# Mixing and gated MLP on one core: own buffers for the first x pieces, the second-stage table in six groups, and the exponent clamps moved from VectorE to ScalarE

## The chip, the core and the metric

One core of a Trainium2 chip. The metric is the device time of one execution in microseconds (us), which for one core is the time of that core. Executions of one kernel mostly agree within 0.3%. Medians are given, and ratios with a 95% interval.

Names: PE is TensorE's matmul, PEld its weight load, DVE is VectorE, ACT is ScalarE, POOL is GpSimd, SP is the engine that issues most DMAs. The granted clock is the share of its full clock that TensorE had in a stretch, as the profile records it. L392 is line 392 of the kernel concerned, so the same statement has different numbers in different kernels.

## The reference, cut to what matters

```python
X = np.fft.fft(x, axis=1)          # x: (8, 3008, 256) float32
X = np.fft.fft(X, axis=2)
h = X.real.astype(np.float32).reshape(24064, 256) @ w_in    # w_in: (256, 2048), float64
g = h * np.clip(h + 3.0, 0.0, 6.0) / 6.0
out = (g @ w_out).astype(np.float32)                        # w_out: (2048, 256), float64
```

The weights arrive as float64. The kernel doesn't compute in it: it takes the two 32-bit halves of each number and builds a float32 with integer operations. That is "the conversion" below: 16 tiles of 128x512.

## The kernel before

The batches go in four pairs. Of a pair, 32 rows come in eight chunks of four and are folded with their mirror rows (fetched by a gather, an indirect DMA), go through a first Fourier stage on TensorE (stage 1), are copied to z on ScalarE, stored to DRAM, read back as g, and go through stage 2 and the gated MLP. Later pairs do their first stage beside the MLP of the pair ahead. The first pair has nothing to hide behind, and its start also has to convert the weights. ScalarE and VectorE run their operations in the order in which the program emits them; the traces below show it (in the changed kernel a ScalarE operation whose input is ready at 85.3 us starts at 89.33, behind two copies emitted before it).

```python
PR = 94                                   # partitions of an x tile
xpool = ...tile_pool(name="xpool", bufs=2)

def load_x(pr, c):                        # one chunk
    xt = xpool.tile([PR, 2 * XC, D], F32, tag="x", name="xt")
    nc.gpsimd.dma_start(out=xt[:, 0:n, :], in_=rows[...])             # rows
    nc.gpsimd.indirect_dma_start(out=xt[:, XC:, :]..., in_=x_r, ...)  # mirror rows: the gather
...
def narrow(st, o):                        # the conversion, all on VectorE
    ts(top[:], hi, 0xFFFFF, 0x100000, op0=AL.bitwise_and, op1=AL.bitwise_or)
    ts(low[:], lo, 8, 0xFFFFFF, op0=AL.logical_shift_right, op1=AL.bitwise_and)
    stt(frac[:], low[:], 2.0 ** -24, top[:], op0=AL.mult, op1=AL.add)
    ts(ex[:], hi, 20, 0x7FF, op0=AL.logical_shift_right, op1=AL.bitwise_and)
    ts(ex[:], ex[:], 1023.0 - 127.0, 0.0, op0=AL.subtract, op1=AL.max)   # clamp
    ts(ex[:], ex[:], 255.0, 2.0 ** 23, op0=AL.min, op1=AL.mult)          # clamp
    stt(ex[:], hi, -2 ** 31, ex[:], op0=AL.bitwise_and, op1=AL.bitwise_or)   # sign
    stt(o, frac[:], 2.0 ** -20, ex[:].bitcast(F32), op0=AL.mult, op1=AL.mult)
...
for c in range(NXC):                      # eight chunks of the first pair
    for part, eng in enumerate((nc.gpsimd, nc.vector)):
        fold(first, c, part, eng)         # part 0 on GpSimd, part 1 (y) on VectorE
    if c + 2 < NXC: load_x(first, c + 2)
    for i in range(XC // 2):
        stage1(first, c, i)               # TensorE matmul, then nc.scalar.copy(z, ps)
    narrow_w_in(c)
    if c + 2 < NWI: load_w_in(c + 2)
    if c % 2: fold_w_in(c // 2)           # TensorE: w_in folded with the dimension transform
# ... then two w_out conversions; the other six beside the first eight gate steps
```

Of the kernel before, what the change touches and what calls it, by code (L numbers as in the profile page):

```python
# [7 lines left out]
F32 = mybir.dt.float32  # L8
# [40 lines left out]
def kernel(  # L49
# [30 lines left out]
    xpool = ctx.enter_context(tc.tile_pool(name="xpool", bufs=2))  # L80
# [21 lines left out]
    T = consts.tile([P, 2, NK1, 2, N2], F32, name="T")  # L102
# [14 lines left out]



    def load_x(pr, c):  # L120
        xt = xpool.tile([PR, 2 * XC, D], F32, tag="x", name="xt")
# [3 lines left out]
        if n < XC:  # L125
# [3 lines left out]
            out=xt[:, XC:, :].rearrange("p n d -> p (n d)"), out_offset=None, in_=x_r,  # L129
            in_offset=bass.IndirectOffsetOnAxis(ap=IX[:, i:i + 1], axis=0),  # L130
        )
        pr.x[c] = xt

    def fold(pr, c, part, eng):
        xt = pr.x[c]
        n = XC if c < NXC - 1 else XC - 1
        a, r = xt[:, 0:n, :], xt[:, 2 * XC - 1:2 * XC - 1 - n:-1, :]
# [7 lines left out]
        lo, hi = xt[:, 0:XC, 1:P], xt[:, 0:XC, D - 1:P:-1]  # L145
# [3 lines left out]
        if n < XC:  # L149
            h = xt[:, XC, :]  # L150
            tt(y[:, XC, 1:P], h[:, 1:P], h[:, D - 1:P:-1], op=AL.add)
            tt(y[:, XC, P + 1:D], h[:, 1:P], h[:, D - 1:P:-1], op=AL.subtract)
            eng.tensor_copy(y[:, XC, 0:P + 1:P], h[:, 0:P + 1:P])
            eng.tensor_copy(y[:, n, 0:P + 1:P], xt[:, n, 0:P + 1:P])
# [46 lines left out]
    def stage2(pr, gr, i):  # L201
# [5 lines left out]
        for u in range(2):  # L207
            kk = 2 * i + u
            for blk in range(2):
                nc.tensor.matmul(ps[:, blk, 2 * u:2 * u + 2], g[:, kk, blk * P:(blk + 1) * P],  # L210
                                 T[:, blk, gr * 2 * KK + kk], start=True, stop=True)
        nc.scalar.copy(pr.q[gr][:, :, 4 * i:4 * i + 4, :], ps[:])

    def stage2n_mul(pr, gr):

        shape = [P, 2 * KK, 2 * N2]
        m = spool.tile(shape, F32, tag="m", name="m")
        t0 = T[:, 0, gr * 2 * KK:(gr + 1) * 2 * KK].rearrange("p k b n -> p k (b n)")
        nc.gpsimd.tensor_tensor(m[:], t0, pr.g[gr][:, :, P:P + 1].to_broadcast(shape), op=AL.mult)
        pr.pr[gr] = m  # L220

    def stage2n_sum(pr, gr):
        m = pr.pr.pop(gr)
        ps = bank([P, 2 * TB], "ps3")
        nc.tensor.matmul(ps[:], ones[:], m[:].rearrange("p k n -> p (k n)"), start=True, stop=True)  # L225
# [128 lines left out]
    for c in range(2):  # L354
        load_x(first, c)
# [7 lines left out]
    def load_w(src, dst):  # L363
        if not wide:
            nc.sync.dma_start(out=dst, in_=src)
            return None
        st = wpool.tile([P, 2 * WB], I32, tag="st", bufs=3, name="st")
# [6 lines left out]
    def narrow(st, o):  # L374


        if st is None:
            return
        words = st[:].rearrange("p (n two) -> p n two", two=2)
        lo, hi = words[:, :, 0], words[:, :, 1]  # L380
        ts, stt = nc.vector.tensor_scalar, nc.vector.scalar_tensor_tensor
        top = wpool.tile([P, WB], I32, tag="top", name="top")
        low = wpool.tile([P, WB], I32, tag="low", name="low")
        ex = wpool.tile([P, WB], I32, tag="ex", name="ex")
        frac = wpool.tile([P, WB], F32, tag="frac", name="frac")
        ts(top[:], hi, 0xFFFFF, 0x100000, op0=AL.bitwise_and, op1=AL.bitwise_or)
        ts(low[:], lo, 8, 0xFFFFFF, op0=AL.logical_shift_right, op1=AL.bitwise_and)  # L387
        stt(frac[:], low[:], 2.0 ** -24, top[:], op0=AL.mult, op1=AL.add)  # L388
        ts(ex[:], hi, 20, 0x7FF, op0=AL.logical_shift_right, op1=AL.bitwise_and)
        ts(ex[:], ex[:], 1023.0 - 127.0, 0.0, op0=AL.subtract, op1=AL.max)  # L390
        ts(ex[:], ex[:], 255.0, 2.0 ** 23, op0=AL.min, op1=AL.mult)
        stt(ex[:], hi, -2 ** 31, ex[:], op0=AL.bitwise_and, op1=AL.bitwise_or)  # L392
        stt(o, frac[:], 2.0 ** -20, ex[:].bitcast(F32), op0=AL.mult, op1=AL.mult)

    w_in = {}

    def load_w_in(j):
        n, i = j // 2, j % 2
        w = wpool.tile([P, WB], F32, tag="w", bufs=5, name="w_in")
        w_in[n, i] = w, load_w(moe_w_in[i * P:(i + 1) * P, n * WB:(n + 1) * WB], w[:])  # L400

    def narrow_w_in(j):
        w, st = w_in[j // 2, j % 2]
        narrow(st, w[:])


    w_out = {}

    def load_w_out(j):
        w = wpool.tile([P, WB], F32, tag="w", bufs=5, name="w_out")  # L410
        rows = moe_w_out[2 * j * P:2 * (j + 1) * P, :].rearrange("(c p) d -> p c d", p=P)
        w_out[j] = w, load_w(rows, w[:].rearrange("p (c d) -> p c d", c=2))

    def narrow_w_out(j):
        w, st = w_out[j]
        narrow(st, w[:])

    def mix_w_out(j):
        bs = [w_out[j + i * (NWO // 2)][0][:].rearrange("p (c q h e) -> h p c q e", c=2, h=2, e=DH) for i in range(2)]
# [14 lines left out]
    for j in range(2):  # L434
        load_w_in(j)
    for b in range(2):
        nc.vector.memset(T[(1 - b) * N2:(2 - b) * N2, :, :, b], 0.0)
        nc.scalar.dma_start(out=T[b * N2:(b + 1) * N2, :, :, b], in_=c_stage2)
# [3 lines left out]
    def fold_w_in(n):  # L442

        cs = slice(n * 512, (n + 1) * 512)
        for blk in range(2):
            ps = bank([P, 512], "wps")
            for i in range(2):
                nc.tensor.matmul(ps[:], C[:, i, blk * P:(blk + 1) * P], w_in[n, i][0][:],
# [3 lines left out]
        for j in range(512 // P):  # L452
            for i in range(2):
                nc.tensor.matmul(ps[:, j:j + 1], w_in[n, i][0][:, j * P:(j + 1) * P], C[:, i, D:D + 1],
                                 start=(i == 0), stop=(i == 1))
        nc.scalar.copy(WN[:, n * (512 // P):(n + 1) * (512 // P)], ps[:, 0:512 // P])

    for c in range(NXC):
        for part, eng in enumerate((nc.gpsimd, nc.vector)):
            fold(first, c, part, eng)  # L460
        if c + 2 < NXC:
            load_x(first, c + 2)
        for i in range(XC // 2):
            stage1(first, c, i)
        narrow_w_in(c)
        if c + 2 < NWI:
            load_w_in(c + 2)
        if c % 2:
            fold_w_in(c // 2)
    ORDER = [0, NWO // 2, 1, NWO // 2 + 1, 2, NWO // 2 + 2, 3, NWO // 2 + 3]  # L470
    for j in ORDER[0:2]:
        load_w_out(j)
# [6 lines left out]
    for j in range(2):  # L479
        narrow_w_out(ORDER[j])  # L480
        load_w_out(ORDER[j + 2])
    mix_w_out(0)
    starting[0] = False

# [4 lines left out]
    def beside(p):  # L489
# [6 lines left out]
        if p == 0:  # L496
            for j in range(2, NWO):
                put(j - 2, narrow_w_out, ORDER[j])
                if j + 2 < NWO:
                    put(j - 2, load_w_out, ORDER[j + 2])  # L500
# [63 lines left out]
def _tables(B, S, D):  # L564
# [14 lines left out]
    for b in range(2):  # L579
# [21 lines left out]
        "c_stage2": t.reshape(N2, 2, NK1, N2).astype(np.float32),  # L601
# [33 lines left out]
```

## Time and profile before

| | before |
|---|---|
| median, us | 2097.04 (2094.95 to 2097.82) |
| last z copy of the first pair starts at | 102.85 |
| first gate step (the first `s` on VectorE) at | 120.09 |
| last weight conversion ends at | 191.93 |
| TensorE full from | 196.84 |

I call the time up to the first gate step "half one" and the eight slow gate steps after it "half two".

The next lines are from the list of waits of the first 125 us (who waited for whom: us in total, times, the longest). They are what makes half one long: GpSimd waits for the gathers, VectorE for GpSimd.

```profile
DVE y L146 <- POOL xt L141: 40.9, 6, 15.5
POOL xt L140 <- DMA xt<-in_x_dram,IX: 40.2, 6, 15.3
```

The stretches between GpSimd's take-up of chunks 0, 2, 4 and 6 (length, then busy us and counts of PE, PEld, DVE, ACT and POOL, the granted clock, the DMA share and GB/s): each pair of chunks costs 21 us, in which no engine is busy for more than 14.05.

```profile
23.57:44.72 21.15, 12.91 (x22) 4.82 (x22) 14.05 (x22) 3.19 (x6) 9.35 (x9) 1.00 0.57 152
44.72:65.82 21.10, 13.71 (x39) 6.27 (x38) 13.62 (x22) 3.96 (x8) 9.63 (x8) 0.68 0.56 159
65.82:86.60 20.78, 12.96 (x32) 5.51 (x31) 11.31 (x22) 3.51 (x7) 10.01 (x10) 0.67 0.57 158
```

### The profile page before, as it was taken

How to read it: one execution, taken by the hardware profiler on the slowest of the kernel's cores; microseconds unless marked ns; L12 is line 12 of the kernel's file. 1: busy time of each engine (PE TensorE's matmuls, PEld its weight loads, DVE VectorE, ACT ScalarE, POOL GpSimd, SP SyncE). 2: the span in 40 equal slices, each digit the busy share in tenths (PEclk: the TensorE clock that was granted, in tenths of full speed). 3: DMA queues.
4: the chain of work that ended last, by engine and by line, in shares of the span. 5: the costliest groups of instructions: out<-in, count | busy, mean ns of one | idle time of the engine just before them, and what ended most of it. 6: DMA issues, size and time to landing. Idle time of an engine off the chain costs nothing.

```text
span 2095.7 us, 28082 instructions
## 1 busy us (share of the span) xinstructions
PE 1985.9 (95%) x9136; PEld 1698.7 (81%) x9136; DVE 1495.8 (71%) x2768; ACT 671.6 (32%) x1157; POOL 1474.1 (70%) x1637
## 2 busy tenths in 40 slices
PE   3666999999999999999999999999999999999997
PEld 1355888888888888888888888888888888888886
DVE  4588676777677677667677667777677777777775
ACT  1122333333333333333333333333333333333332
POOL 3333887788667788778767787787866766766765
PEclk9678999999999999999999999999999999999999
DMA  6430121112101112112101111111020010010000
GB/s 160 133 110 10 43 54 48 50 37 49 28 21 34 43 33 61 47 38 52 35 21 30 42 38 43 42 51 47 23 48 11 14 26 21 16 26 21 16 16 19
DMA packets 163377, 86.81 MB, mean 41 GB/s; under 512 B 138496, under 2 KB 151040, under 8 KB 163232
## 3 DMA queue, kind: packets, MB, share of 16 engines
q1 hardware_dynamic: 128896, 58.71, 11.4%
q0 software_dynamic: 28160, 24.73, 4.4%
q10 hardware_dynamic: 6176, 1.57, 0.4%
q8 instruction: 74, 1.21, 0.3%
q14 instruction: 71, 0.58, 0.1%
HBM read 47.65 MB, written 37.22 MB: 40 GB/s over the span
## 4 chain that ended last, share of the span: by engine, by line
PE 88%; DVE 5%; DMA 4%; ACT 1%; POOL 1%; issue 1%; SPq 0%; DVEq 0%; POOLq 0%; ACTq 0%
PE acc L308 52%; PE v L254 15%; PE u L254 15%; DMA xt<-in_x_dram,IX 3%; PE ps L210 2%; PE ps L182 2%; DVE a L286 1%; PE ps L225 1%; ACT t L283 1%; DVE u L267 1%; DVE s L259 0%; DVE frac L388 0%; DVE low L387 0%; DMA g<-zd 0%; DVE ex L392 0%
## 5 line engine op out<-in xcount | busy, mean ns | idle before, releaser
L298 POOL TENSOR_TENSOR c<-a 128x512 f32<-128x512 f32 (+1 forms) x384 | 479.2, 1248 | 447.2 <-DVE a L286 257.2
L308 PE MATMUL acc<-c,G 128*128 128x256 f32 (+1 forms) x3072 | 714.0, 375 | 0.0
L308 PEld LDWEIGHTS acc<-c,G 128*128 128x128 f32 x3072 | 579.7, 191 | 73.9
L283 ACT ACTIVATE t<-u,half 128x512 f32<-128x512 f32 (+2 forms) x416 | 272.2, 654 | 1102.5 <-DVE u L267 1090.8
L259 DVE SCALAR_TENSOR_TENSOR s<-qn,WN,u 128x256 f32<-128x256 f32 x768 | 334.7, 477 | 365.1 <-PE u L254 364.5
L308 PE MATMUL acc<-a,G 128*128 128x256 f32 (+1 forms) x2304 | 557.5, 379 | 0.0
L308 PEld LDWEIGHTS acc<-a,G 128*128 128x128 f32 x2304 | 439.8, 192 | 58.7
L254 PE MATMUL v<-q,W 128*128 128x256 f32 x1536 | 402.3, 385 | 31.7 <-DVE a L286 31.7
L254 PE MATMUL u<-q,W 128*128 128x256 f32 x1536 | 395.0, 379 | 0.0
L254 PEld LDWEIGHTS v<-q,W 128*128 128x128 f32 x1536 | 292.6, 192 | 80.3 <-issue 35.3
L254 PEld LDWEIGHTS u<-q,W 128*128 128x128 f32 x1536 | 287.9, 190 | 65.8 <-issue 20.7
L286 DVE SCALAR_TENSOR_TENSOR a<-t,u 128x512 f32<-128x512 f32 (+2 forms) x416 | 266.2, 646 | 99.2 <-ACT t L283 94.0
L298 POOL TENSOR_TENSOR c<-a,c 128x256 f32<-128x256 f32 (+1 forms) x384 | 276.2, 719 | 30.1
L298 POOL TENSOR_TENSOR c<-c,a 128x256 f32<-128x256 f32 (+1 forms) x384 | 274.9, 716 | 30.1
L267 DVE TENSOR_TENSOR u<-s,v 128x512 f32<-128x512 f32 (+1 forms) x384 | 263.0, 685 | 41.1 <-PE v L254 1.3
L283 ACT ACTIVATE t<-v,half 128x512 f32<-128x512 f32 (+1 forms) x384 | 256.9, 669 | 5.5 <-DVE v L273 4.5
L273 DVE TENSOR_TENSOR v<-v,s 128x512 f32<-128x512 f32 (+1 forms) x384 | 257.7, 671 | 1.1
L286 DVE SCALAR_TENSOR_TENSOR a<-t,v 128x512 f32<-128x512 f32 (+1 forms) x416 | 255.1, 620 | 0.4 <-ACT t L283 0.2
L182 PE MATMUL ps<-y,F 94*96 94x512 f32 x120 | 73.7, 712 | 59.9 <-DVE y L148 53.8
L298 POOL TENSOR_TENSOR r<-w,e 128x256 f32<-128x256 f32 (+1 forms) x96 | 92.2, 981 | 3.8
L314 ACT COPY e<-acc 128x512 f32<-128x512 f32 (+1 forms) x192 | 86.3, 540 | 2.9 <-PE acc L308 2.8
L182 PEld LDWEIGHTS ps<-y,F 94*96 94x96 f32 x120 | 20.7, 186 | 80.3 <-issue 34.3
(68 smaller groups left out, 856.3 us busy)
## 6 DMA issues: line engine op xcount, KB each, us to landing
out_dram<-o SPq DMA_DIRECT2D x736, 32.0 KB, 1.6
zd<-z SPq DMA_DIRECT2D x32, 384.0 KB, 3.0
g<-zd SPq DMA_DIRECT2D x48, 256.0 KB, 3.9
xt<-in_x_dram POOLq DMA_DIRECT2D x28, 376.0 KB, 4.0
st<-in_moe_w_in_dram SPq DMA_DIRECT2D x8, 512.0 KB, 10.2
st<-in_moe_w_out_dram SPq DMA_DIRECT2D x8, 512.0 KB, 6.0
T<-in_c_stage_dram ACTq DMA_DIRECT2D x2, 768.0 KB, 25.5
xt<-in_x_dram POOLq DMA_DIRECT2D x4, 282.0 KB, 3.4
```

The source lines that it names most:

```text
L182: nc.tensor.matmul(ps[0:PZ], F[0:PR, 0:PZ], y[:, 2 * i:2 * i + 2, :], start=True, stop=True)
L210: nc.tensor.matmul(ps[:, blk, 2 * u:2 * u + 2], g[:, kk, blk * P:(blk + 1) * P], T[:, blk, gr * 2 * KK + kk], start=True, stop=True)
L225: nc.tensor.matmul(ps[:], ones[:], m[:].rearrange("p k n -> p (k n)"), start=True, stop=True)
L254: nc.tensor.matmul(ps[:, i], W1[:, blk, f * P:(f + 1) * P], q[:, blk, of:of + KC], start=True, stop=True)
L259: nc.vector.scalar_tensor_tensor(s[:, i].rearrange("p k n -> p (k n)"), qn[:, of * N2:(of + KC) * N2], WN[:, f:f + 1], u[:, i].rearrange(" ...
L267: nc.vector.tensor_tensor(u[:, :, 0:ns], s[:, :, 0:ns], v[:, :, 0:ns], op=AL.add)
L273: nc.vector.tensor_tensor(v[:, :, 0:nm], v[:, :, 0:nm], s[:, :, 0:nm], op=AL.subtract)
L283: nc.scalar.activation(t, h, AF.Relu, bias=half[:], scale=scale)
L286: nc.vector.scalar_tensor_tensor(dst, t, 1.0, h, op0=AL.min, op1=AL.mult)
L298: nc.gpsimd.tensor_tensor(out, in0, in1, op=AL.add)
L308: nc.tensor.matmul(ch.acc[i // 2][:, i % 2, 0:ch.n], G[:, i, fc, :], mv, start=(fc == 0 and i % 2 == 0), stop=(fc == NF - 1), skip_group_c ...
L314: nc.scalar.copy(ch.e[:, k:i + 1, 0:ch.n], ch.acc[i // 2][:, 0:i + 1 - k, 0:ch.n])
```

## The change

The intent: fetch the first pair's x much earlier, by using buffers that the MLP needs only later; keep the 1.5 MB table out of the first microseconds; take work from VectorE, which bounds half two. The core of the diff, with cuts:

```diff
+    def x_tile(pr, i):
+        pool, tag = xpool, "x"                                  # xpool: bufs=4, tiles of half the size
+        if pr.p == 0 and 4 <= i < 13:
+            pool, tag = ((apool, "a"), (cpool, "c"), (spool, "t"))[(i >= 8) + (i >= 11)]
+        return pool.tile([PR, XC, D], F32, tag=tag, name="xt")
...
-        ts(ex[:], ex[:], 1023.0 - 127.0, 0.0, op0=AL.subtract, op1=AL.max)
-        ts(ex[:], ex[:], 255.0, 2.0 ** 23, op0=AL.min, op1=AL.mult)
+        ts(ex[:], hi, 20, 0x7FF, op0=AL.logical_shift_right, op1=AL.bitwise_and)
+        nc.scalar.activation(w[:], ex[:], AF.Relu, bias=bias[:, 0:1], scale=1.0)
+        nc.scalar.activation(w[:], w[:], AF.Relu, bias=bias[:, 1:2], scale=-1.0)
+        nc.scalar.activation(ex[:], w[:], AF.Identity, bias=bias[:, 2:3], scale=-2.0 ** 23)
+        ...                                                     # top, low, frac, sign, product as before
...
+    for j in range(2):
+        narrow_next(j)                    # two conversions ahead of the loop
+    fold_w_in(0)
     for c in range(NXC):
         ...fold(first, c, part, eng)
-        if c + 2 < NXC: load_x(first, c + 2)
+        if c + 3 < NXC: load_x(first, c + 3)
         ...stage1(first, c, i)            # with the two z copies on ScalarE
-        narrow_w_in(c)
-        if c % 2: fold_w_in(c // 2)
+        narrow_next(c + 2)
+        if c % 2 and c < NWI - 2: fold_w_in(c // 2 + 1)
+        if c == NXC - 4: load_t(0)        # table: group 0 here, 1 to 5 after the loop
```

More of the change, by code (lines that the diff above doesn't have):

```diff
@@ L79 @@
     consts = ctx.enter_context(tc.tile_pool(name="consts", bufs=1))
-    xpool = ctx.enter_context(tc.tile_pool(name="xpool", bufs=2))
+    xpool = ctx.enter_context(tc.tile_pool(name="xpool", bufs=4))
     ypool = ctx.enter_context(tc.tile_pool(name="ypool", bufs=2))
@@ L101 @@
     IX = consts.tile([PR, NP * NXC], I32, name="IX")
-    T = consts.tile([P, 2, NK1, 2, N2], F32, name="T")
+    T = consts.tile([P, 2, NG, 2, 2 * KK, N2], F32, name="T")
     C = consts.tile([P, 2, D + 1], F32, name="C")
@@ L115, in __init__ @@
             self.g, self.q, self.qn, self.pr = {}, {}, {}, {}
+    def x_tile(pr, i):
[3 more added lines that the diff above has]
+        return pool.tile([PR, XC, D], F32, tag=tag, name="xt")
     def load_x(pr, c):
-        xt = xpool.tile([PR, 2 * XC, D], F32, tag="x", name="xt")
+        xt, xr = x_tile(pr, 2 * c), x_tile(pr, 2 * c + 1)
         rows = x_pn[pr.p * PR:(pr.p + 1) * PR]
@@ L128, in load_x @@
         nc.gpsimd.indirect_dma_start(
-            out=xt[:, XC:, :].rearrange("p n d -> p (n d)"), out_offset=None, in_=x_r,
+            out=xr[:].rearrange("p n d -> p (n d)"), out_offset=None, in_=x_r,
             in_offset=bass.IndirectOffsetOnAxis(ap=IX[:, i:i + 1], axis=0),
         )
-        pr.x[c] = xt
+        pr.x[c] = xt, xr
     def fold(pr, c, part, eng):
-        xt = pr.x[c]
+        xt, xr = pr.x[c]
         n = XC if c < NXC - 1 else XC - 1
-        a, r = xt[:, 0:n, :], xt[:, 2 * XC - 1:2 * XC - 1 - n:-1, :]
+        a, r = xt[:, 0:n, :], xr[:, XC - 1:(XC - 1 - n) if n < XC else None:-1, :]
         tt = eng.tensor_tensor
@@ L144, in fold @@
         pr.y[c] = y
-        lo, hi = xt[:, 0:XC, 1:P], xt[:, 0:XC, D - 1:P:-1]
+        lo, hi = xt[:, :, 1:P], xt[:, :, D - 1:P:-1]
         tt(y[:, 0:XC, 1:P], lo, hi, op=AL.add)
@@ L149, in fold @@
         if n < XC:
-            h = xt[:, XC, :]
+            h = xr[:, 0, :]
             tt(y[:, XC, 1:P], h[:, 1:P], h[:, D - 1:P:-1], op=AL.add)
@@ L210, in stage2 @@
                 nc.tensor.matmul(ps[:, blk, 2 * u:2 * u + 2], g[:, kk, blk * P:(blk + 1) * P],
-                                 T[:, blk, gr * 2 * KK + kk], start=True, stop=True)
+                                 T[:, :, gr, blk, kk], start=True, stop=True)
         nc.scalar.copy(pr.q[gr][:, :, 4 * i:4 * i + 4, :], ps[:])
     def stage2n_mul(pr, gr):
-        shape = [P, 2 * KK, 2 * N2]
+        shape = [P, 2 * KK, 2, N2]
         m = spool.tile(shape, F32, tag="m", name="m")
-        t0 = T[:, 0, gr * 2 * KK:(gr + 1) * 2 * KK].rearrange("p k b n -> p k (b n)")
-        nc.gpsimd.tensor_tensor(m[:], t0, pr.g[gr][:, :, P:P + 1].to_broadcast(shape), op=AL.mult)
+        t0 = T[:, :, gr, 0].rearrange("p b k n -> p k b n")
+        gn = pr.g[gr][:, :, P:P + 1].unsqueeze(2).to_broadcast(shape)
+        nc.gpsimd.tensor_tensor(m[:], t0, gn, op=AL.mult)
         pr.pr[gr] = m
@@ L224, in stage2n_sum @@
         ps = bank([P, 2 * TB], "ps3")
-        nc.tensor.matmul(ps[:], ones[:], m[:].rearrange("p k n -> p (k n)"), start=True, stop=True)
+        nc.tensor.matmul(ps[:], ones[:], m[:].rearrange("p k b n -> p (k b n)"), start=True, stop=True)
         pr.qn[gr] = qpool.tile([P, 2 * TB], F32, tag="qn", name="qn")
@@ L353 @@
     nc.vector.tensor_copy(IX[:], F[0:PR, 5 * PZ:])
-    for c in range(2):
-        load_x(first, c)
     nc.sync.dma_start(out=C[:], in_=c_dim.rearrange("(h p) d -> p h d", p=P))
@@ L361, with load_w @@
     WB = 512
-    def load_w(src, dst):
-        if not wide:
-            nc.sync.dma_start(out=dst, in_=src)
-            return None
-        st = wpool.tile([P, 2 * WB], I32, tag="st", bufs=3, name="st")
+    def load_w(src):
+        tag, bufs, dt = ("st", 3, I32) if wide else ("w", 4, F32)
+        st = wpool.tile([P, WB * (1 + wide)], dt, tag=tag, bufs=bufs, name=tag)
         o = st[:].bitcast(moe_w_in.dtype)
@@ L372, in load_w, with narrow @@
         return st
-    def narrow(st, o):
-        if st is None:
-            return
+    def narrow(st):
+        if not wide:
+            return st
         words = st[:].rearrange("p (n two) -> p n two", two=2)
@@ L381, in narrow @@
         ts, stt = nc.vector.tensor_scalar, nc.vector.scalar_tensor_tensor
+        ex = wpool.tile([P, WB], I32, tag="ex", bufs=2, name="ex")
+        w = wpool.tile([P, WB], F32, tag="w", bufs=4, name="w")
         top = wpool.tile([P, WB], I32, tag="top", name="top")
         low = wpool.tile([P, WB], I32, tag="low", name="low")
-        ex = wpool.tile([P, WB], I32, tag="ex", name="ex")
-        frac = wpool.tile([P, WB], F32, tag="frac", name="frac")
+        ts(ex[:], hi, 20, 0x7FF, op0=AL.logical_shift_right, op1=AL.bitwise_and)
@@ L386, in narrow @@
+        nc.scalar.activation(w[:], ex[:], AF.Relu, bias=bias[:, 0:1], scale=1.0)
+        nc.scalar.activation(w[:], w[:], AF.Relu, bias=bias[:, 1:2], scale=-1.0)
+        nc.scalar.activation(ex[:], w[:], AF.Identity, bias=bias[:, 2:3], scale=-2.0 ** 23)
         ts(top[:], hi, 0xFFFFF, 0x100000, op0=AL.bitwise_and, op1=AL.bitwise_or)
         ts(low[:], lo, 8, 0xFFFFFF, op0=AL.logical_shift_right, op1=AL.bitwise_and)
-        stt(frac[:], low[:], 2.0 ** -24, top[:], op0=AL.mult, op1=AL.add)
-        ts(ex[:], hi, 20, 0x7FF, op0=AL.logical_shift_right, op1=AL.bitwise_and)
@@ L390, in narrow @@
-        ts(ex[:], ex[:], 1023.0 - 127.0, 0.0, op0=AL.subtract, op1=AL.max)
-        ts(ex[:], ex[:], 255.0, 2.0 ** 23, op0=AL.min, op1=AL.mult)
+        frac = top[:].bitcast(F32)
+        stt(frac, low[:], 2.0 ** -24, top[:], op0=AL.mult, op1=AL.add)
         stt(ex[:], hi, -2 ** 31, ex[:], op0=AL.bitwise_and, op1=AL.bitwise_or)
-        stt(o, frac[:], 2.0 ** -20, ex[:].bitcast(F32), op0=AL.mult, op1=AL.mult)
-    w_in = {}
+        stt(w[:], frac, 2.0 ** -20, ex[:].bitcast(F32), op0=AL.mult, op1=AL.mult)
@@ L397, in load_w_in @@
+        return w
+    w_in, w_out = {}, {}
     def load_w_in(j):
         n, i = j // 2, j % 2
-        w = wpool.tile([P, WB], F32, tag="w", bufs=5, name="w_in")
-        w_in[n, i] = w, load_w(moe_w_in[i * P:(i + 1) * P, n * WB:(n + 1) * WB], w[:])
-    def narrow_w_in(j):
-        w, st = w_in[j // 2, j % 2]
-        narrow(st, w[:])
-    w_out = {}
-    def load_w_out(j):
-        w = wpool.tile([P, WB], F32, tag="w", bufs=5, name="w_out")
-        rows = moe_w_out[2 * j * P:2 * (j + 1) * P, :].rearrange("(c p) d -> p c d", p=P)
-        w_out[j] = w, load_w(rows, w[:].rearrange("p (c d) -> p c d", c=2))
@@ L414, in narrow_w_out @@
-    def narrow_w_out(j):
-        w, st = w_out[j]
-        narrow(st, w[:])
+        w_in[n, i] = load_w(moe_w_in[i * P:(i + 1) * P, n * WB:(n + 1) * WB])
+    def load_w_out(j):
+        w_out[j] = load_w(moe_w_out[2 * j * P:2 * (j + 1) * P, :].rearrange("(c p) d -> p c d", p=P))
     def mix_w_out(j):
-        bs = [w_out[j + i * (NWO // 2)][0][:].rearrange("p (c q h e) -> h p c q e", c=2, h=2, e=DH) for i in range(2)]
+        bs = [w_out[j + i * (NWO // 2)][:].rearrange("p (c q h e) -> h p c q e", c=2, h=2, e=DH) for i in range(2)]
@@ L433, with load_t @@
     NWI, NWO = 2 * FF // WB, NFC // 2
-    for j in range(2):
-        load_w_in(j)
+    ORDER = [i * (NWO // 2) + j for j in range(NWO // 2) for i in range(2)]
+    def load_t(gr):
+        for b in range(2):
+            nc.sync.dma_start(out=T[b * N2:(b + 1) * N2, b, gr], in_=c_stage2[:, gr])
+    for j in range(3):
+        load_w_in(j)
+    for c in range(3):
+        load_x(first, c)
+    bias = consts.tile([P, 3], F32, name="bias")
+    for i, v in enumerate((127.0 - 1023.0, 255.0, 255.0 * 2 ** 23)):
+        nc.vector.memset(bias[:, i:i + 1], v)
     for b in range(2):
-        nc.vector.memset(T[(1 - b) * N2:(2 - b) * N2, :, :, b], 0.0)
-        nc.scalar.dma_start(out=T[b * N2:(b + 1) * N2, :, :, b], in_=c_stage2)
+        nc.vector.memset(T[(1 - b) * N2:(2 - b) * N2, b], 0.0)
     nc.vector.memset(half[:], 0.5)
@@ L447, in fold_w_in @@
             for i in range(2):
-                nc.tensor.matmul(ps[:], C[:, i, blk * P:(blk + 1) * P], w_in[n, i][0][:],
+                nc.tensor.matmul(ps[:], C[:, i, blk * P:(blk + 1) * P], w_in[n, i][:],
                                  start=(i == 0), stop=(i == 1))
@@ L453, in fold_w_in, with narrow_next @@
             for i in range(2):
-                nc.tensor.matmul(ps[:, j:j + 1], w_in[n, i][0][:, j * P:(j + 1) * P], C[:, i, D:D + 1],
+                nc.tensor.matmul(ps[:, j:j + 1], w_in[n, i][:, j * P:(j + 1) * P], C[:, i, D:D + 1],
                                  start=(i == 0), stop=(i == 1))
         nc.scalar.copy(WN[:, n * (512 // P):(n + 1) * (512 // P)], ps[:, 0:512 // P])
+    def narrow_next(j):
+        if j < NWI:
+            w_in[j // 2, j % 2] = narrow(w_in[j // 2, j % 2])
+        else:
+            w_out[ORDER[j - NWI]] = narrow(w_out[ORDER[j - NWI]])
+        j += 3
+        if j < NWI:
+            load_w_in(j)
+        elif j - NWI < NWO:
+            load_w_out(ORDER[j - NWI])
+    for j in range(2):
+        narrow_next(j)
+    fold_w_in(0)
     for c in range(NXC):
@@ L460 @@
             fold(first, c, part, eng)
-        if c + 2 < NXC:
-            load_x(first, c + 2)
+        if c + 3 < NXC:
+            load_x(first, c + 3)
         for i in range(XC // 2):
             stage1(first, c, i)
-        narrow_w_in(c)
-        if c + 2 < NWI:
-            load_w_in(c + 2)
-        if c % 2:
-            fold_w_in(c // 2)
-    ORDER = [0, NWO // 2, 1, NWO // 2 + 1, 2, NWO // 2 + 2, 3, NWO // 2 + 3]
-    for j in ORDER[0:2]:
-        load_w_out(j)
+        narrow_next(c + 2)
+        if c % 2 and c < NWI - 2:
+            fold_w_in(c // 2 + 1)
+        if c == NXC - 4:
+            load_t(0)
     load_g(first, 0)
@@ L478 @@
     stage2n_sum(first, 0)
-    for j in range(2):
-        narrow_w_out(ORDER[j])
-        load_w_out(ORDER[j + 2])
     mix_w_out(0)
+    for gr in range(1, NG):
+        load_t(gr)
     starting[0] = False
@@ L497, in beside @@
             for j in range(2, NWO):
-                put(j - 2, narrow_w_out, ORDER[j])
-                if j + 2 < NWO:
-                    put(j - 2, load_w_out, ORDER[j + 2])
+                put(j - 2, narrow_next, NWI + j)
                 if j % 2:
@@ L600, in _tables @@
         "c_stage1": np.pad(f, ((0, 2), (0, 0))).astype(np.float32),
-        "c_stage2": t.reshape(N2, 2, NK1, N2).astype(np.float32),
+        "c_stage2": t.reshape(N2, 2, NK1 // 4, 4, N2).swapaxes(1, 2).astype(np.float32),
         "c_dim": d.astype(np.float32),
```

## The prediction

> **What bounds the kernel now.** I read the page's 40 slices first, then the table of stretches, then the timeline of the first 200 us.
>
> ```profile
> PE   3666999999999999999999999999999999999997
> PEclk9678999999999999999999999999999999999999
> ...
> 127.50:196.84 69.34, 42.64 (x141) 33.78 (x140) 65.31 (x97) 12.56 (x25) 27.76 (x25) 0.80 0.11 34
> 196.84:2095.70 1898.86, 1878.22 (x8822) 1631.49 (x8822) 1357.77 (x2545) 637.40 (x1092) 1404.22 (x1569) 1.00 0.14 34
> ```
>
> The first two lines are TensorE's busy tenths and granted clock; the others are busy us (and counts) of PE, PEld, DVE, ACT, POOL, then clock, DMA share, GB/s. From 197 us to the end TensorE is busy 1878 of 1899 us, and the change removes no matmul: that part is fixed. Only the first 197 us can move. They have two halves.
>
> Half one, 0 to about 104 us: eight chunks of x are fetched, folded, put through stage 1, and the float64 weights are converted on VectorE. The timeline (start, duration, engine, line, what; in brackets the idle time before it and its releaser) shows one turn:
>
> ```profile
> 56.04 0.16 DVE L148 TENSOR_TENSOR y<-xt 94x8 f32<-94x8 f32 x1
> ...
> 57.64 1.68 POOL L128 DMA_INDIRECT xt<-in_x_dram,IX  x1 [0.30 <-issue]
> 58.38 0.58 ACT L183 COPY z<-ps 96x512 f32<-96x512 f32 x1 [6.32 <-PE ps L182]
> ...
> 60.09 0.58 ACT L183 COPY z<-ps 96x512 f32<-96x512 f32 x1 [1.13 <-PE ps L182]
> 60.32 0.69 DVE L393 SCALAR_TENSOR_TENSOR w_in<-frac,ex 128x512 f32<-128x512 f32 x1
> ...
> 65.82 1.25 POOL L140 TENSOR_TENSOR xt<-xt 94x508 f32<-94x508 f32 x1 [6.50 <-DMA xt<-in_x_dram,IX]
> 73.83 1.61 POOL L140 TENSOR_TENSOR xt<-xt 94x508 f32<-94x508 f32 x1 [1.20 <-DMA xt<-in_x_dram,IX]
> ```
>
> A gather issued at 57.64 is usable at 73.83: 16.2 us. It could not be issued sooner, because with two x buffers it waits for VectorE to have read the chunk two back (56.04). So two chunks cost about 21 us: GpSimd takes them up at 23.57, 44.72, 65.82, 86.60. The stage ends when the last z copy ends, 103.43.
>
> Half two, 120 to 197 us: eight gate steps, six with a w_out conversion. VectorE is busy 65.3 of 69.3 us while TensorE is at 42.6: VectorE bounds it.
>
> **What the Trainium skill says.**
> (1) "DMA: Bandwidth & Descriptors", section "Why a DMA increments its semaphore by 16 and not by 1": a DMA runs on the largest k up to 16 that divides the outer dimension, so a gather of 94 partitions gets two engines, and successive ones get the next engines in turn. The trace agrees: in the undisturbed gather of 218 us nearly all of its 94 packets (4 KB, 159 ns) go in two streams and end at 229.5. Hence latency, not bandwidth, limits x: more gathers in flight should help.
> (2) "TensorE: Matmul & The Clock Gate", "What's actually happening": half speed until some 3.4 us of work. Agrees: a stage-1 matmul pair takes 1.7 us here, 0.86 in the steady part.
> (3) "ScalarE: Activation LUTs", "What ACT_TABLE_LOAD costs": an ACTIVATE with a pointer bias takes about 280 + 0.833 N ns, 707 at N=512. The trace has 687 for such a Relu, which I use.
> (4) "SBUF — State Buffer", "Who interferes with whom": VectorE's two-port operations and GpSimd lock each other out. Agrees: the same tensor_scalar takes 0.42 us alone and 1.49 beside GpSimd's combine.
>
> **The change part by part.**
>
> x pieces. Thirteen of the first pair's 16 pieces get a buffer that nobody else holds; the last three reuse pieces freed long before. Chunks are requested three ahead, straight after GpSimd's own fold. Three 16 us latencies overlap: estimate 16/3 = 5.4 us per chunk instead of 10.5. If x alone set the pace, all would be in by about 55 us. x leaves the path.
>
> Table in six groups. Its 1.5 MB no longer load at the start (two DMAs, 25.5 us to landing, 256-byte packets) but as 12 DMAs with 2 KB runs, group 0 during chunk 4, the rest near the end of the stage. The first x chunk, 23.4 us before, should land at 15 to 18 (estimate). The matmuls read two runs of 64 columns instead of one of 128; the 24 GpSimd products keep 512 elements. I count zero for both.
>
> Clamps on Scalar. Per conversion VectorE loses two tensor_scalar (0.43 us each alone, mean 0.81 and 0.78 in half two). ScalarE gains three dependent activations: 3 x 0.69 plus handovers = 2.2 us. VectorE covers part of that with top, low and frac, about 1.5 us alone, then **waits**.
>
> That wait is where I choose. ScalarE takes work in order, and in half one the three clamps are emitted after the two z copies of the same chunk. So VectorE's conversion of chunk c now cannot end before stage 1 of chunk c is through TensorE and copied. Before, it ran beside them. The new ring is VectorE fold, TensorE stage 1, ScalarE z, ScalarE clamps, VectorE rest, next fold, all in series:
> - A chunk without w_in folding: fold y 1.45, y to last z copy 4.4 (27.26 to 31.67), clamps 2.2, two remaining VectorE operations 1.5: 9.55 us.
> - A chunk behind a w_in folding: the folding ends 6.1 us after the conversion (5.8 at 40.3 to 46.1 before, plus a little cold clock), stage 1 then warm 1.85, z 0.7, clamps 2.2, rest 1.5: 12.3 us.
> - Two chunks: **21.9 us, against 21.1 before.** The x wait is replaced by a wait through ScalarE of the same size.
>
> Now the chain from the start. VectorE is free after the table memsets at 10.4. Two early conversions of 0.45 + 2.2 + 1.5 = 4.1 us end at 18.6. Chunks 0 and 1: 18.6 + 12.3 + 9.55 = 40.4. Two pairs: + 43.8 = 84.2. Last pair: 84.2 + 12.3 + 1.45 + 5.3 (last chunk, y to z, before: 98.1 to 103.4) = 103.3, plus about 1.5 for GpSimd collisions: **104.8 instead of 103.4**. Its conversion ends 3.7 us later, 108.5.
>
> Then g is loaded. SP must first issue a weight load that waits for that conversion, so g is issued at about 109 instead of 107. But only one weight load stands before it, not two with three more behind, so it lands in 5.5 us (estimate; 3.9 is the median over the kernel) instead of 7.3: 114.5 against 114.05. The first two w_out conversions are done by then, so VectorE, held by the first mix until 120.18 before, starts at 114.5 + 5.5 = 120.0. **Half one: gain 0.2 us**, that is nothing.
>
> Half two. A conversion took 6.1 us in the plain steps (138.85 to 144.97) and 7.8 where GpSimd also folds or multiplies (150.57 to 158.39). Without the clamps: 0.42 + 1.45 + 1.0 + 1.0 + 0.7 + 0.7 = 5.3, and about 6.4. The clamps hide here: VectorE is held 3.4 us by the GpSimd collisions, ScalarE needs 2.2 and has nothing in front of it. Saved: 3 x 0.8 + 3 x 1.4 = **6.6 us**, all of it on the path.
>
> Sum: 2096.6 - 0.2 - 6.6 = 2089.8. I lean to 2087, since half one is the sum of many small terms and its x side has much to give if the ring is shorter than I think.
>
> **Rivals.**
> A: the ring does not bind, and VectorE's own work does: fold 1.45 plus conversion some 4.3 plus collisions, say 7.4 us per chunk. From 25 us that is 25 + 59 = 84 for the end of z, a gain of 19; with half two and the earlier start of g, about 2068. For it: x really is early, and the author's aim. Against it: the order on ScalarE, and the 4.4 us from y to z that each turn shows.
> B: the ring is longer: TensorE cold in the folding and in stage 1 behind it (+1.6 us each, four times), ScalarE late in half two. Half one loses 6 to 10 us and eats the rest: 2093 to 2099.
> C: x still binds, because gathers share engines or queue behind the weights. Then half one stays at 103 and only half two gains: 2090, the same time for another reason.
>
> **Range and chances.** A and B span 2068 to 2099. I predict 2087, range 2068 to 2099. Faster by 2% needs 2054.7, a gain of 42 us; even A with half two gives 29, so 0.03. Slower by 2% needs 42 us lost in stages that total 197: 0.01. Within 2%: 0.96.
>
> **What would show it.** Right: no GpSimd idle behind the x gather after the first chunk; VectorE idle in front of the sign operation (bitwise or into ex) with a ScalarE releaser, some 3 to 6 us per chunk in half one and about none in half two; chunk pairs 21 to 23 us apart on VectorE; last z copy near 104; TensorE solid from about 190 instead of 197. Wrong: gather waits still there (C); VectorE nearly full before 100 us and the last z near 85 (A). A changed length of the part in which TensorE is solid (1899 us) would break the frame of the whole argument.

## The result, and the profile after

| | before | after |
|---|---|---|
| median, us | 2097.04 | 2099.32 (2096.26 to 2101.81) |
| ratio to before | | 1.0012, interval 0.9994 to 1.0029: the same |
| last z copy starts at | 102.85 | 111.06 |
| first gate step at | 120.09 | 127.78 |
| first gate step to the last conversion's end | 71.8 | 64.4 |
| TensorE full from | 196.84 | 197.06 |

A ratio is the mean time of one kernel's runs over that of the other's runs of the same rounds, so it is not quite the ratio of the medians. The four runs of the changed kernel spread over 5.5 us, those of the kernel before over 2.9. The times of events are from the one profiled execution of each kernel. Of the changed kernel that was its fastest run (2096.26), so the events show where time was won and lost, not the last 2 us of the medians.

The change won 7.4 us in half two and lost 7.7 in half one. The list of waits of the changed kernel, first 125 us:

```profile
DVE ex L399 <- ACT ex L394: 45.3, 10, 8.5
...
POOL xt L147 <- DMA xt<-in_x_dram,IX: 23.9, 4, 12.3
...
DVE y L153 <- POOL xt L148: 7.0, 1, 7.0
```

VectorE's wait for GpSimd and its gathers has gone from 40.9 us to 7.0, all of it in the first chunk. In its place stands a wait of 45.3 us that did not exist: the sign operation (L399) waits for the third ScalarE clamp (L394). The timeline of chunk 5 (counted from 0), which comes after the last GpSimd fold and so is undisturbed, shows why:

```profile
84.80 0.17 DVE L155 TENSOR_TENSOR y<-xt 94x8 f32<-94x8 f32 x1
84.88 0.42 DVE L391 TENSOR_SCALAR ex<-st 128x512 int32<-128x512 int32 x1
...
86.00 0.69 DVE L398 SCALAR_TENSOR_TENSOR top<-low,top 128x512 f32<-128x512 int32 x1
87.14 0.58 ACT L190 COPY z<-ps 96x512 f32<-96x512 f32 x1 [4.90 <-PE ps L189]
...
88.85 0.58 ACT L190 COPY z<-ps 96x512 f32<-96x512 f32 x1 [1.12 <-PE ps L189]
89.33 0.72 ACT L392 ACTIVATE w<-ex,bias 128x512 f32<-128x512 int32 x1
...
91.59 0.69 DVE L399 SCALAR_TENSOR_TENSOR ex<-st,ex 128x512 int32<-128x512 int32 x1 [4.90 <-ACT ex L394]
```

The exponent is ready at 85.3, and ScalarE is idle. But next in ScalarE's queue stand the two z copies, which wait for TensorE; the clamp starts only at 89.33. VectorE has done the rest at 86.7 and stands still until 91.59. Its next fold comes behind that, and the next stage 1 behind the fold.

The stretches between ends of conversions 3, 5, 7 and 9 (the two ahead of the loop are 0 and 1), one pair of chunks each. The last was cut at 115.14, 0.09 before conversion 9 ended:

```profile
46.20:70.77 24.57, 14.43 (x32) 6.14 (x32) 13.72 (x20) 7.80 (x13) 14.10 (x12) 0.57 0.53 146
70.77:93.01 22.24, 13.49 (x32) 6.06 (x32) 8.71 (x19) 7.80 (x13) 0.00 (x0) 0.73 0.33 95
93.01:115.14 22.13, 12.34 (x38) 6.93 (x38) 9.17 (x23) 7.80 (x13) 0.00 (x0) 0.65 0.27 83
...
197.06:2094.50 1897.44, 1876.87 (x8822) 1630.51 (x8822) 1358.06 (x2545) 638.80 (x1092) 1406.19 (x1569) 1.00 0.15 34
```

The two pairs in which GpSimd is idle take 22.2 and 22.1 us. The first listed, in which it is busy for 14.10 us, takes 24.6, and the pair before it (chunks 0 and 1, from the end of conversion 1 at 18.23 to 46.20) took 28.0. The last line shows the part with TensorE full, as long as before (1898.86).

### The profile page after: what moved, and what is told of

Same layout as the page of the kernel before. It is cut to its first block, busy times and chain, and to the rows that moved or that the text cites. A ratio compares the mean times of both kernels' runs of the same rounds, so it can differ in the third digit from the quotient of the medians.

```text
span 2094.5 us, 28106 instructions
## 1 busy us (share of the span) xinstructions
PE 1984.0 (95%) x9136; PEld 1696.0 (81%) x9136; DVE 1483.3 (71%) x2739; ACT 707.1 (34%) x1205; POOL 1478.3 (71%) x1637
## 3 DMA queue, kind: packets, MB, share of 16 engines
q1 hardware_dynamic: 129856, 60.28, 12.7%
## 4 chain that ended last, share of the span: by engine, by line
PE 90%; DVE 5%; ACT 2%; DMA 1%; issue 1%; POOL 0%; SPq 0%; DVEq 0%; POOLq 0%; ACTq 0%
PE acc L316 52%; PE v L262 15%; PE u L262 15%; PE ps L189 3%; PE ps L217 2%; DMA xt<-in_x_dram,IX 1%; PE ps L233 1%; DVE a L294 1%; PE wps L453 1%; DVE ex L399 1%; ACT t L291 1%; DVE u L275 1%; DVE s L267 0%; DVE w L400 0%; DVE o L342 0%
## 5 line engine op out<-in xcount | busy, mean ns | idle before, releaser
L189 PE MATMUL ps<-y,F 94*96 94x512 f32 x120 | 68.3, 664 | 34.2 <-DVE y L155 28.1
L342 DVE STREAM_TRANSPOSE o<-r 128x256 f32<-128x256 f32 (+1 forms) x192 | 72.4, 415 | 6.4 <-POOL r L306 6.4
```

The lines of the kernel that those rows point to most:

```text
L189: nc.tensor.matmul(ps[0:PZ], F[0:PR, 0:PZ], y[:, 2 * i:2 * i + 2, :], start=True, stop=True)
L342: nc.vector.transpose(o[:, 0:n // DH, h], ch.r[:, m, h, 0:n].rearrange("p (j i) -> p j i", i=DH))
```

## The experiments

**Theory.** Half one of the changed kernel is paced by a ring: VectorE's fold, TensorE's stage 1, ScalarE's z copies, ScalarE's clamps, the rest of VectorE's conversion, the next fold. Moving the clamps behind the z copies closed it; the x buffers opened another ring (buffer, gather, fold) of the same length.
**Rivals.** The gathers and GpSimd's collisions with VectorE pace it, and ScalarE is only where the wait shows. Or the gather wait was hidden anyway and the x buffers bought nothing. No run has the table groups alone, or the two conversions ahead of the loop alone; what each of them is worth stays open.

Event times in the table are taken as above; "half two" is from the first gate step to the last conversion's end. (The expectations give the end of the last z copy, 0.58 later, and count their second half up to TensorE full: 76.8 us before, 69.3 in the change.)

| kernel | last z copy | first gate step | half two | median, us | ratio to before |
|---|---|---|---|---|---|
| before | 102.85 | 120.09 | 71.8 | 2097.04 | 1 |
| the change | 111.06 | 127.78 | 64.4 | 2099.32 | 1.0012 |
| vec_clamps | 86.31 | 102.78 | 70.6 | 2077.03 | 0.9908 |
| early_clamps | 92.89 | 107.75 | 64.4 | 2076.40 | 0.9907 |
| before_clamps | 108.88 | 132.79 | 66.1 | 2103.26 | 1.0039 |
| four_acts | 117.22 | 134.30 | 64.4 | 2103.30 | 1.0040 |
| clamps_ahead | 79.34 | 93.13 | 64.4 | 2061.62 | 0.9832 |
| ahead_two_x | 102.03 | 116.19 | 64.4 | 2087.48 | 0.9956 |
| no_pool_fold (wrong values) | 103.63 | 119.43 | 64.4 | 2089.53 | 0.9967 |
| before_gather96 | 77.37 | 94.07 | 71.5 | 2069.64 | 0.9868 |
| after_gather96 | 108.01 | 125.01 | 64.8 | 2094.14 | 0.9991 |
| ahead_gather96 | 78.99 (two merged) | 95.43 | 64.8 | 2061.78 | 0.9830 |
| ahead_gather96_two_x | 74.80 | 90.09 | 64.8 | 2058.51 | 0.9820 |

Every result but that of no_pool_fold was correct.

### vec_clamps: the change without its third part

```diff
-        nc.scalar.activation(w[:], ex[:], AF.Relu, ...)      # and the two behind it
+        ts(ex[:], ex[:], 1023.0 - 127.0, 0.0, op0=AL.subtract, op1=AL.max)
+        ts(ex[:], ex[:], 255.0, 2.0 ** 23, op0=AL.min, op1=AL.mult)
```

> The changed kernel with the two clamps of the conversion back on VectorE, everything else of the change kept. Theory (the ring VectorE fold, stage 1, z copy, ScalarE clamps, VectorE rest paces the first half): the ring opens, a chunk costs VectorE some 1.45 + 4.3 + 1.5 = 7.3 us, last z copy near 83 us instead of 111.6, first gate step near 97 instead of 127.8; the second half goes back to 77 us from 69; TensorE solid from about 174; total near 2076. Rival (gathers and GpSimd collisions pace it, ScalarE is only where the wait shows): last z copy stays above 105, total 2100 to 2106.

It took 2077.03, with the last z copy at 86.31; the first gate step, at 102.78, came 6 us later than expected. The theory holds: more work on VectorE, and half one ends 25 us earlier. The clamps' place on ScalarE, not the gathers, made half one long. Half two goes back to 70.6 us, so the two effects of the clamps are separate.

### before_clamps: the third part alone

```diff
-        ts(ex[:], ex[:], 1023.0 - 127.0, 0.0, ...)           # in the kernel before, both clamps
+        nc.scalar.activation(o, ex[:], AF.Relu, ...)         # and the two behind it
```

> The kernel before with nothing but the clamps on ScalarE. Theory: the ring of 22 us for two chunks runs beside the gather latency (16.2 + 2.3 us from one fold to the next but one), so it hides the gather wait: pairs near 22 us, last z copy near 110, second half about 69 us, total 2096 to 2103, as the whole change. Rival (gather wait and ring add up): 2115 or more.

It took 2103.26, at the upper edge of what the theory gave and far from the rival's 2115. With vec_clamps this makes a table of two by two. By the ratios, times 2097: clamps alone 8 us slower, the rest of the change alone (buffers, table, the two early conversions) 19 us faster, both together 2.5 us slower. If the parts added up, the sum would be 11 us faster. The last z copies say the same: 6.0 us later, 16.5 sooner, together 8.2 later. The parts don't add up, because each opens or closes one of two rings that run side by side, and the longer one sets the pace.

Not all of the 12.7 us by which this kernel's gate step is late are the ring of the eight chunks: 6.0 are there at the last z copy, the other 6.7 come behind it. Here two w_out conversions follow the loop, and their clamps queue on ScalarE behind stage 2's copies, which wait for g:

```profile
122.87 0.59 ACT L227 COPY qn<-ps 128x512 f32<-128x512 f32 x1 [0.28 <-PE ps L225]
123.36 0.72 ACT L387 ACTIVATE w_out<-ex,bias 128x512 f32<-128x512 int32 x1
...
125.62 0.69 DVE L393 SCALAR_TENSOR_TENSOR ex<-st,ex 128x512 int32<-128x512 int32 x1 [9.03 <-ACT ex L389]
```

In the changed kernel these two conversions are done in chunks 6 and 7.

### four_acts: the suspected cost made larger

```diff
         nc.scalar.activation(w[:], w[:], AF.Relu, bias=bias[:, 1:2], scale=-1.0)
+        nc.scalar.activation(w[:], w[:], AF.Relu, bias=bias[:, 3:4], scale=1.0)   # bias 0
...                                # bias gets a fourth column
```

> The changed kernel with a fourth, dependent ScalarE operation in each conversion that changes no value (0.76 us). Theory: 0.76 us more for each of the eight chunks of the first half, nothing in the second: last z copy near 117 to 118, total 6 us more than the changed kernel, near 2105. Rival (ScalarE not on the path): no change, below 2101.

The last z copy moved from 111.06 to 117.22, by 6.2 us; half two stayed at 64.4. That it is just eight times 0.77 is in part luck: GpSimd took up the first x at 24.61 in this run (22.92 in the change), so that the first fold was 1.7 us late already; the seven chunks from there to the last fold add 4.5, that is 0.64 each. The total rose by 5.9 us by the ratios (1.0040 against 1.0012), by 4.0 by the medians. ScalarE's clamps are on the path in half one, and hidden in half two.

### early_clamps: same work, other order (a miss by 12 us)

```diff
     for c in range(NXC):
+        head_next(c + 2)       # exponent on VectorE and the three clamps on ScalarE
         ...fold, load_x, stage1 with its z copies...
         narrow_next(c + 2)     # top, low, frac, sign, product
```

> The changed kernel with the exponent and the three ScalarE clamps of a conversion emitted ahead of the fold and the z copies of the same chunk, so that they don't queue behind them. Theory: same work on every engine, ring open: last z copy near 80, first gate step near 93, second half 69 us, TensorE solid from about 162, total near 2064, and VectorE's wait for the clamps nearly gone. Rival (gathers and collisions): within 5 us of the changed kernel's 2099.

2076.40: it wins 22 us by the ratios (23 by the medians) by nothing but an order, but the expected 2064 was missed. The timeline shows what is left of the wait. In every other chunk the clamps now stand behind ScalarE's copies of the w_in folding, which were emitted in the chunk before:

```profile
49.51 0.16 ACT L475 COPY WN<-wns 128x4 f32<-128x4 f32 x1 [1.09 <-PE wns L473]
49.57 0.72 ACT L388 ACTIVATE w<-ex,bias 128x512 f32<-128x512 int32 x1
...
51.83 1.48 DVE L413 SCALAR_TENSOR_TENSOR ex<-st,ex 128x512 int32<-128x512 int32 x1 [3.96 <-ACT ex L390]
```

### clamps_ahead: the clamps in front of those copies too

```diff
+    head_next(2)               # once, ahead of the loop; the call at the loop's top is gone
...
         narrow_next(c + 2)
+        if c + 3 < NXC + 2:
+            head_next(c + 3)   # for the next chunk, ahead of the copies of the folding
         if c % 2 and c < NWI - 2:
             fold_w_in(c // 2 + 1)
```

> The changed kernel with a conversion's exponent and clamps emitted one chunk earlier than in the last try: behind the rest of the conversion before, and so ahead of the copies of the w_in folding too. Theory (the last try's remaining 12 us are the clamps queued behind the copies of the w_in folding in every other chunk): pairs of chunks 13 to 14 us instead of 16.5, last z copy near 80, total near 2065. Rival (what is left is TensorE and VectorE work, not the queue on ScalarE): no better than the last try's 2076.

2061.62, with the last z copy at 79.34. The remaining wait was the queue: VectorE waited 17.3 us for the clamps in the last try (first 100 us), and 5.4 here (first 90 us). This kernel has all three parts of the change and is 1.7% faster than the kernel before.

### ahead_two_x: the same with the x buffers of before

```diff
-        if pr.p == 0 and 4 <= i < 13:      # nine more buffers, three chunks ahead
+        if False:                          # two chunks of buffers
...                                         # and the loads two chunks ahead instead of three
```

> The kernel of the run before this with x back to two chunks of buffers, loaded two ahead. Theory: with the ring open, the gather latency of 16 us and the two buffers pace it again, 20 to 21 us for a pair as in the kernel before, last z copy near 100, second half 69 us: 2085 to 2091. Rival (the x buffers never mattered): as fast as the run before.

2087.48, as the theory gave. With the ScalarE ring open the gather ring is back, and the x buffers are worth 26 us. In the change itself they show no gain: before_clamps has neither them nor the table groups, and its last z copy came 2.2 us sooner than the change's (108.88 against 111.06). That the change is faster than it by 6 us in total comes from behind the last z copy, where before_clamps does its two w_out conversions.

### no_pool_fold: how much were GpSimd's collisions?

```diff
-        for part, eng in enumerate((nc.gpsimd, nc.vector)):
-            fold(first, c, part, eng)
+        fold(first, c, 1, nc.vector)       # first pair only; wrong values on purpose
```

> The changed kernel without GpSimd's two fold additions for the first pair of batches (wrong values on purpose for those rows). Theory (of the 7 us by which the first half ran longer than predicted, most are VectorE operations held up by GpSimd's fold in chunks 0 to 3): the first fold y starts 2.3 us sooner and the pair of chunks 2 and 3 takes 22 us instead of 24.6, last z copy near 104 instead of 111.6, total 6 to 7 us less, near 2092. Rival (cold TensorE and the late first gather make up the 7 us): 2 to 3 us less.

The first z copy came 2.3 us sooner (25.52 against 27.81), the last 7.4 sooner, so 5.1 us lie in between: VectorE operations held up by GpSimd. The changed kernel's own trace agrees: on the ring, six VectorE operations of chunks 0 to 3 take 5.3 us more than the same operations take undisturbed. Of the 2.3 us ahead of the first z copy some 1.3 have another reason: the first w_in folding took 6.3 us in this run and 7.6 in the change. The pair of chunks 2 and 3 took 22.7 us (22 expected). The total is 9 us lower by the ratios, more than expected. The run lies close to my prediction for half one: last z copy done at 104.2 (predicted 104.8), first gate step at 119.4 (predicted 120.0). But the prediction had 1.5 us of collisions in it, and this run has none, and foldings that took up to 7.5 us instead of 6.1; so the closeness is in part luck.

### before_gather96: why was a gather 16 us long?

```diff
-    IX = consts.tile([PR, NP * NXC], I32, name="IX")           # PR = 94
+    IX = consts.tile([PR + 2, NP * NXC], I32, name="IX")       # two unused rows
-        xt = xpool.tile([PR, 2 * XC, D], F32, tag="x", name="xt")
+        xt = xpool.tile([PR + 2, 2 * XC, D], F32, tag="x", name="xt")
...                                                            # plain loads and folds keep rows 0 to 93
```

> The kernel before with nothing changed but the gather of x over 96 partitions instead of 94 (the two extra rows fetch row 0 and are not used). Theory (the 16 us are long because 94 rows go on two DMA engines): 96 rows spread over 16 engines, a gather lands in 4 to 6 us, pairs of chunks fall from 21 to some 14.5 us (VectorE), last z copy near 80, total near 2074. Rival (the 16 us are GpSimd's building of descriptors or sharing with the weights' loads): 2090 or more.

2069.64: two more rows, and nothing else, make the kernel before 1.3% faster. The summary of the x tile (first 110 us of before, then first 90 us of this kernel; plain loads and gathers together):

```profile
DMA to landing us min/median/max: 3.8/14.3/19.4
```

```profile
DMA to landing us min/median/max: 3.7/5.6/13.0
```

The gathers alone took 15.9 us (median) before and 5.0 now. The completion events in the traces show why. Of the gather issued at 28.70 in the kernel before, 14 of 16 came by 32.2 and the other two at 44.2 and 44.6, while the 16 of the plain load just ahead of it came between 31.0 and 31.6. With 96 rows all 16 of a gather came within 1.2 us (issued at 190.58, events from 194.3 to 195.5).

The pairs of chunks are 15.9 us apart now, against 14.5 expected (VectorE's first conversions end at intervals of 7.9), with VectorE busy for 20.67 of 21.15 us in the stretch from 23.57 to 44.72, where it was busy for 14.05 before. So the bound that the change attacked with nine buffers came from the number 94.

### after_gather96: is the gather still the bound in the change?

> The changed kernel with the x gathers over 96 partitions instead of 94, nothing else. Theory (in the changed kernel the gathers no longer pace the first half, the ring through ScalarE does): only the first chunk gains, 2 to 5 us in all, pairs stay at 22 us, total 2094 to 2098. Rival (gathers still pace it): the same 27 us that the 96 rows gave the kernel before, near 2072.

The same edit on the changed kernel (on its tiles xt and xr) gives 2094.14, that is 4 us by the ratios, with intervals that overlap, where the kernel before won 27. The pairs from chunk 2 on take 21.7 to 22.8 us: in the changed kernel the gathers don't pace them. The small gain is not the first chunk's, as the theory had it. GpSimd takes it up at 13.09, but then its fold holds up the two early conversions (the second ends at 21.79 instead of 18.23), and the first z copy comes at 28.93, 1.1 us later than in the change. What is shorter is the time from there to the last z copy, by 4.2 us; GpSimd is through with its folds at 44.0 here and at 68.5 in the change, so fewer of them can meet the ring.

### ahead_gather96 and ahead_gather96_two_x: what beats both

> The kernel with the clamps one chunk ahead (2061.6) and the gathers over 96 partitions. Theory (its first half is now paced by VectorE and TensorE, 13 us a pair, and only its first chunk waits for x): 2 to 5 us less, 2056 to 2060. Rival (gathers still cost each pair something): below 2053.

> The same with two chunks of x buffers, loaded two ahead, as in the kernel before. Theory (the extra x buffers only hid the slow gather): within 3 us of the run before, against the 26 us that they were worth with the gather over 94 rows. Rival (buffers are worth something in themselves): 2070 or more.

The first was a miss: 2061.78, no gain over clamps_ahead. Its timeline shows a VectorE operation that takes 0.69 us elsewhere:

```profile
37.81 7.09 DVE L414 SCALAR_TENSOR_TENSOR w<-top,ex 128x512 f32<-128x512 f32 x1
...
38.01 1.29 POOL L147 TENSOR_TENSOR xt<-xt 94x508 f32<-94x508 f32 x1
...
43.48 0.85 POOL L148 TENSOR_TENSOR xt<-xt 94x381 f32<-94x381 f32 x1
```

With x there early and buffers to spare, GpSimd runs three chunks' folds back to back, and VectorE's product of two SBUF tensors lasts until GpSimd is through. With two chunks of buffers GpSimd has to wait between folds, and that kernel is the fastest of all: 2058.51, ratio 0.9820 (0.9803 to 0.9836; the interval overlaps that of ahead_gather96). The extra x buffers only served to hide the slow gather; with a fast one they are worth nothing or cost a little.

## Why the prediction was right or wrong

The measured 2099.3 lies just above the range's end of 2099. The mechanism (x off the path, a ring through ScalarE of about the same length in its place) was right, and it is shown; what failed is the sum for half one. It put the end of the last z copy at 104.8, and it came at 111.64; instead of a gain of 0.2 us up to the gate step there was a loss of 7.7. Two terms were too small, and nearly all of the 6.8 us lie in the first two pairs of chunks (28.0 and 24.6 us instead of 21.9).

- *The fixed part, TensorE full for 1899 us*: right, 1897.4.
- *x leaves the path, and a ring through ScalarE of the same length replaces it*: right. "Two chunks: 21.9 us" measured 22.2 and 22.1 where GpSimd was quiet; VectorE's wait for the clamps was 45.3 us. vec_clamps, early_clamps, clamps_ahead and four_acts show that it is the order on ScalarE.
- *Half two, 6.6 us saved*: right, 7.4, and the clamps are hidden there (four_acts).
- *"Plus about 1.5 for GpSimd collisions"*: **this step failed.** no_pool_fold puts the collisions between the first and the last z copy at 5.1 us, the trace of the change at 5.3. In the changed kernel GpSimd no longer waits for buffers and runs its folds and DMA issues close together in chunks 0 to 3, where the two remaining VectorE operations and the fold y, all on the ring, meet them. In chunk 3 (the fold's operations take 0.68, 0.68 and 0.17 us undisturbed):

```profile
59.85 1.35 POOL L147 TENSOR_TENSOR xt<-xt 94x508 f32<-94x508 f32 x1 [3.85 <-DMA xt<-in_x_dram,IX]
60.00 1.74 DVE L154 TENSOR_TENSOR y<-xt 94x508 f32<-94x508 f32 x1
61.16 1.52 POOL L148 TENSOR_TENSOR xt<-xt 94x508 f32<-94x508 f32 x1
61.67 1.05 DVE L155 TENSOR_TENSOR y<-xt 94x8 f32<-94x8 f32 x1
```

- *"The folding ends 6.1 us after the conversion"*: **failed too.** From the end of the conversion to the start of the folding's last copy it took 7.6, 7.3, 6.9 and 6.1 us, 3.5 us more in all. TensorE ran slower: its granted clock was 0.62, 0.65 and 0.75 in the last three; the kernel before has 1.00, 0.82 and 0.87 in its first three foldings, which took 5.7 to 5.8. (For the first the record of the clock says 1.00, yet its weight loads last 0.33 us as in the slow ones, against 0.19.) No run tests this term alone.
- *"The first x chunk ... should land at 15 to 18"*: **failed too.** GpSimd took it up at 22.92, hardly earlier than before (23.57). The table had gone, but a third x chunk and a third weight tile had come in its place. Whether these held it up is not shown; with the same loads and a gather over 96 rows GpSimd starts at 13.09 (after_gather96). It cost little: stage 1 began at 26.68 instead of the 24.7 that followed from the two early conversions, but the slow first folding would have held it until 25.8, so 0.9 us are x's. The three terms (3.6, 3.5 and 0.9 us) come to 8.0, against a miss of 6.8; the other terms of the sum were about 1 us too large together.
- *From g to the gate step, 5.5 us*: g landed 6.0 us after its first issue (5.5 estimated), and the gate step came 6.6 us later. The matmul pair of the sum took 1.92 us against 1.02 before: TensorE's granted clock was 0.65 in the last 3.3 us ahead of the gate step, against 0.97 before. In both kernels it began stage 2 at 0.50, after 10.2 us of waiting here and 5.6 before; that the longer wait is the reason is not shown.
- *The choice of 2087 after a sum of 2089.8*: the lean went the wrong way. What speaks for it, "its x side has much to give", is exactly what a ring of equal length withholds.

Of the signs that I named, the wait in front of the sign operation (5.4 us per chunk, leaving out the two conversions ahead of the loop) and its absence in half two came true. The last z copy near 104 did not (111.6), and of the four pairs of chunks only the last two were 21 to 23 us apart. TensorE full from 190 did not come true either (197), nor did GpSimd's freedom from gather waits after the first chunk: three of 3.7 to 4.0 us are left, which hold up nobody.

Of the rivals, A (2068) would have needed the clamps on VectorE: vec_clamps is that kernel in half one (last z copy at 86 against 84), without A's gain in half two. B, the longer ring, is what came (it gave 2093 to 2099): slow foldings, as it said, and about as much from GpSimd, which it did not name.

## What to carry to other kernels

When work moves to an idle engine, look at what stands in front of it in that engine's queue, not at how idle it is: an in-order engine that waits for a matmul is as good as busy, and emitting the moved work earlier costs nothing (here it turned +0.1% into -1.7%). When a wait is removed, look for the second ring of the same length beside it, and test the parts of a change one by one, since they need not add up. And before buying buffers against a long latency, ask why it is long.

## What the Trainium skill lacked or had wrong

- "DMA: Bandwidth & Descriptors", "Why a DMA increments its semaphore by 16 and not by 1": the rule held for the gather, and the page's rules for authors have it too, but neither has a measured cost. It says that SWDGE gives some direct copies all 16 engines with a partition count that 16 does not divide, and so it was for the plain x loads here; the gather over the same 94 partitions got two. 94 to 96 rows took the median landing of the x DMAs from 14.3 to 5.6 us and the kernel from 2096.9 to 2069.6.
- "SBUF — State Buffer", "Who interferes with whom": it says that an instruction with two SBUF inputs contends with GpSimd's reads, but not that VectorE is not let in between GpSimd's instructions. Here one of 0.69 us lasted 7.09 while six fold instructions of GpSimd ran back to back.
- "ScalarE: Activation LUTs", "What ACT_TABLE_LOAD costs": the duration is right within 2% (0.72 us for 512 elements with a pointer bias, 0.707 by the page). The overlap of about 93 ns between back-to-back ACTIVATEs that it states is not there between dependent ones: the clamps start 0.75 to 0.76 us apart (89.33, 90.08, 90.84).
- No page says that work given to ScalarE can stall VectorE through the order on ScalarE's queue; the cost here was 45.3 us of VectorE's time in the first 125.
